# First expert's tokens found by one-hot products, tables joined on GpSimd, put-off sums and a third sum at other steps

## The chip, the cores and the metric

The kernel runs on one core of a Trainium2 chip. TensorE (PE) multiplies, VectorE (DVE) and ScalarE (ACT) move and combine, GpSimd (POOL) does a little arithmetic and issues indirect DMAs, SP issues most plain DMAs. The metric is the device time of one execution in microseconds (us). The median of the runs and their spread are given; one execution was also recorded by the profiler, and all rows below are of that one.

## The reference

Three stages in a row, all in float32. `q`, `k`, `v` are (4, 8, 576, 64), so 2304 tokens of width 512.

```python
# 1. windowed causal attention with a distance bias, 8 heads, window 128
scores = where(mask, q @ k.T / 8 + bias, -1e9)
x = softmax(scores) @ v                         # tokens x 512
# 2. a gated layer, d_ff 1536
x = (sigmoid(x @ w_gate) * (x @ w_val)) @ w_out
# 3. eight experts, each token goes to one
logits = normalize(x) @ normalize(expert_emb).T / tau
expert_idx = argmax(logits); gate_w = softmax(logits)[expert_idx]
for e in range(8):
    m = expert_idx == e
    out[m] = gate_w[m] * (relu(x[m] @ w1[e]) @ w2[e])   # 512 -> 1024 -> 512
```

## The kernel before, in words

**Precision.** Every matmul operand is split into a high part in a short float format and the rest: ScalarE casts the high part (`hi_copy`, line 106), VectorE subtracts it to get the low part (`lo_sub`, line 122), and TensorE does three products (high x high, high x low, low x high). So each weight tile of 128x1024 costs a cast of some 1.05 us on ScalarE and a subtraction of some 1.22 us on VectorE before TensorE can use it.

**Attention and the gated layer.** Attention runs in 36 units, and the gated layer follows in two groups of token blocks (`PAIRS`, called the first and the second group here) for which the products with the weights use a seven-product scheme: sums S1 to S4 of blocks of x, and T1 to T4 of the weights, replace one product in eight. `builds(pair)` makes the sums and their splits: `"S3+"` computes the third sum of the second group (`sum_x`, line 332, one VectorE operation on 128x1024), `"S3"` splits it. `seven(pair, f, ...)` gives the products m1 to m7 of one of the twelve column blocks f with what follows each of them. The result g is not used at once: `keep_g` multiplies gate and value (line 484), stores the blocks A11 to A22 of g to memory and also forms sums of them (S1 to S4, line 465) for the products with `w_out`. Where such a sum isn't needed at once, it is put off: a closure goes into `put_off`, and `catch_up(n, pin)` takes the next one out, computes it on VectorE and stores it (`put`: on SP's queue for the first group, on GpSimd's for the second). Until it is stored, the rows that it reads and writes stay taken. At the end of the first group some sums are left over; the loop over f of the second group (line 883) takes one out after `m3` of each of its first three steps.

**Rows.** Most temporaries of 128x513 floats (`row(name)`) come from one pool `mid` of ten buffers: gate and value blocks, the converted `w_out` (`cvwo`), the routed rows `xr`, the gathered rows `xg`, the results `y`. An instruction that writes a new row waits until the last use of an older one is over, and with a store or a gather that means until the DMA has landed.

**The output product and the routing.** 14 products (`SEQ`) form x2 = g @ w_out, group by group; beside TensorE's work, `AT2` lists what is issued at which step (j, half z, place). As soon as a group of token blocks is ready, it is routed. The groups are b = 3, 5, 1, 7 (four blocks of 128 tokens each) and 0 (two blocks); 7 and 0 are called `LATE`.
- `route_a`, `route_l` compute the logits, the maximum, its index (`ixf`), the softmax weight (written into column 512 of the row, line 1061), and GpSimd writes the rows to `x2_d` in memory (line 1063).
- `route_b` (line 1071) gives each token its place among those of its expert: matmuls of a one-hot `oh` with a triangle of ones (`rk`), then `rank`; from it the address `ai` (line 1095) in a table. GpSimd then scatters the token numbers `ids_sb` to that address by an indirect DMA for each block (line 1102), into one of four tables `tab_d[u]` (u is the block in the group), so that the four scatters don't wait for each other. An empty entry holds the number NT = 2304, above all tokens.
- `places(o, x, c0, q)` reads a column range of all four tables by four DMAs on queue q and joins them by two VectorE operations `min` (lines 954 and 955): an empty entry loses against a token. The result is a list of token numbers.
- `gather` (line 1145) fetches the listed rows of `x2_d` by an indirect DMA on GpSimd. With `upto` it leaves out numbers from there on and the row is cleared first (line 1150).
- `close` runs after `route_b(1)`: it counts the tokens, picks the most loaded expert but the first as second (`by_count`; SP and GpSimd read its number into a register), and then, for expert 0 (two tiles of 128 tokens) and the second one (one tile), calls `places` and `gather`. These first tiles hold tokens of groups 3, 5 and 1 only, so the experts can begin before the groups 7 and 0 are routed; `bump` makes the ranks of the late groups begin behind them.

**The experts.** `transp` turns gathered rows (`tx`), `ffn1` and `ffn2` are the two products, and each result is scattered to the output by an indirect DMA on GpSimd. Expert 0 starts with its two early tiles while groups 7 and 0 are still being routed. After `route_b(0)` the weights of the second expert are converted (`weights(1)`), and `load_col(0)`, `load_col(1)` read the rest of both lists from the tables (into `more`, then `cols`); then come the gathers of these tiles, and from there the experts in turn, each with the next one's weights loaded and converted beside it.

**Order.** Inside `tc.manual_schedule` blocks the listed engines work in the order of the text. Outside, the builder's planner orders the instructions of each engine from their dependences and its own estimates of time; `tc.issue_after(i)` holds instructions until after i in that order, `tc.keep_in_program_order` pins one. At run time every engine, and each of the two queues SP and GpSimd, works strictly in the planned order: an instruction that waits holds up all behind it.

Of the kernel before, what the change touches and what calls it, by code (L numbers as in the profile page):

```python
# [9 lines left out]
F32 = mybir.dt.float32  # L10
F32R = mybir.dt.float32r
BF16 = mybir.dt.bfloat16
# [11 lines left out]
DM = 512  # L24
# [36 lines left out]
def attn_ffn_moe(ctx: ExitStack, tc: tile.TileContext, qkd, vd, wgv, w_out, emb, tau, w1, w2, cst, ids, out):  # L61
# [10 lines left out]
    tab_d = [dram.tile([P * E * TCOL, 1], I32, tag=f"tab_d{y}", name=f"tab_d{y}") for y in range(NTAB)]  # L72
# [21 lines left out]
    tri_f = cs[:, P:2 * P]  # L94
# [522 lines left out]
    nc.sync.dma_start(cs, cst[:, 8 * P:])  # L617
# [214 lines left out]
    bB["S2"]()  # L832
    split_w(1, 0, 1)
    run(2)
    load_wt(1)
# [44 lines left out]
    bB["S3+"]()  # L880
    bB["S3"]()
    WO_AT = [[], [0], [1], [2], [3], [4], [5, 6], [7], [8], [9], [10], []]
    for f in range(KF):
# [6 lines left out]
        if f == 0:  # L890
            bB["A22"]()
            bB["S4+"]()
            bB["S4"]()
# [14 lines left out]
        if f == KF - 1:  # L908
            split_op(0, [0, 1])
        s["m3"]()  # L910
        if f < 3:
            catch_up(pin=True)
# [32 lines left out]
    idt = cp.tile([P, E * TCOL], I32, tag="idt", name="idt")  # L945
    nc.gpsimd.memset(idt, NT)
# [4 lines left out]
    def places(o, x, c0, q):  # L951
        for y, v in enumerate(tab_v):
            q.dma_start(x[:, y, :], v[:, bass.ds(c0, o.shape[1])])
        nc.vector.tensor_tensor(out=x[:, 0:2, :], in0=x[:, 0:2, :], in1=x[:, 2:4, :], op=ALU.min)
        nc.vector.tensor_tensor(out=o, in0=x[:, 0, :], in1=x[:, 1, :], op=ALU.min)
# [9 lines left out]
    tri = cp.tile([P, P], BF16, tag="tri", name="tri")  # L965
    nc.vector.tensor_copy(tri, tri_f)
    one = cp.tile([P, P], BF16, tag="one", name="one")
# [14 lines left out]
    cp.tile([P, 16], I32, tag="pad", name="pad")  # L982
    idx0 = cp.tile([P, 2 * CE], I32, tag="idx0", name="idx0")
    idxs = [cp.tile([P, NTAB, n], I32, tag=f"idxs{e}", name=f"idxs{e}") for e, n in enumerate(EARLY)]
    routed, mark, reg, held = {}, {}, {}, {}
# [85 lines left out]
    def route_b(b):  # L1071
# [13 lines left out]
        nc.vector.tensor_reduce(out=rank, in_=j8, axis=mybir.AxisListType.X, op=ALU.add)  # L1085
        ri = few(nu, "ri", f"ri{b}", dt=I32)
# [13 lines left out]
        for u in range(nu):  # L1100
            t = 2 * b + u
            nc.gpsimd.indirect_dma_start(out=tab_d[u], out_offset=IOA(ap=ai[:, u:u + 1], axis=0),
                                         in_=ids_sb[:, t:t + 1], in_offset=None)
# [24 lines left out]
    def close():  # L1128
# [8 lines left out]
        for e, n in enumerate(EARLY):  # L1137
            reg[e] = nc.gpsimd.value_load(ord_e[0:1, e:e + 1], min_val=0, max_val=E - 1) if e else 0
            places(idx0[:, e * CE:e * CE + n], idxs[e], reg[e] * TCOL, nc.gpsimd)
            for t in range(n):  # L1140
                gather(e, t, idx0[:, e * CE + t:e * CE + t + 1], NE * P)

    xg = {}
# [289 lines left out]
    route_b(0)  # L1433
    behind(0, lambda: weights(1))()
# [17 lines left out]
    for e in range(2):  # L1452
        load_col(e)
# [210 lines left out]
```

## Time and profile before

| what | value |
|---|---|
| runs | 822.89 us median of 3 (819.43 to 824.91) |
| profiled execution | 825.32 us, span of its instructions 823.6 us |
| TensorE busy | 786.6 us (96%), mean granted clock 0.975 |
| VectorE busy | 583.2 us (71%) |
| ScalarE busy | 449.1 us (55%) |
| GpSimd busy | 216.9 us (26%) |
| DMA | 175.77 MB, mean 213 GB/s |

The span is from the first to the last instruction. A granted clock of 1.00 is TensorE's full 2.4 GHz, 0.50 is 1.2 GHz, and a mean over a stretch lies between. PEld is the load of weights into TensorE, which runs beside its products. A row of a timeline gives the start, the length, engine, line, operation, output and inputs by their names in the program, and in brackets the idle time just before it and what ended that.

### The profile page before, as it was taken

To read this page: it belongs to the slowest core of one execution; us is meant where nothing else is said; L and a number is where in the kernel's file an instruction comes from. 1 tells how busy PE (TensorE), PEld (TensorE's weight loads), DVE (VectorE), ACT (ScalarE), POOL (GpSimd) and SP (SyncE) were. 2 spreads that over 40 slices of the span, in tenths; PEclk is the share of its full clock that TensorE was granted. 3 is DMA by queue.
4 is the path that set the end of the run, shared out by engine and by line. 5 is a ranking of instruction groups with operands and counts; after the bars stand their busy time and mean duration, and the time that the engine had idled before them with its cause. 6 is when DMAs were issued, how large, how long until landed. Compare 5 with 4: busy or idle time off the path is not lost. (4 is left out here: it accounts for less than half of the span.)

```text
span 823.6 us, 15796 instructions
## 1 busy us (share of the span) xinstructions
PE 786.6 (96%) x5585; PEld 657.7 (80%) x5585; DVE 583.2 (71%) x1372; ACT 449.1 (55%) x953; POOL 216.9 (26%) x346
## 2 busy tenths in 40 slices
PE   8989999999999889999999999969799999999996
PEld 5768888878888668887787777748579989899995
DVE  7988978889899768897877587618355785456621
ACT  6888766666546445556656677536143543344510
POOL 6756423322000012232200033533503120402100
PEclk9998999999999899999999999979899999999999
DMA  8686478865674489999985596475448745636100
GB/s 273 202 260 218 148 255 280 272 230 195 239 250 172 173 326 352 355 363 377 342 273 181 161 242 207 117 179 129 104 138 295 234 169 184 212 103 229 57 24 19
DMA packets 75714, 175.77 MB, mean 213 GB/s; under 512 B 12499, under 2 KB 20819, under 8 KB 75632
## 3 DMA queue, kind: packets, MB, share of 16 engines
q1 hardware_dynamic: 65264, 145.24, 53.0%
q0 software_dynamic: 10368, 29.50, 10.5%
q8 instruction: 45, 0.74, 0.4%
q14 instruction: 37, 0.30, 0.1%
HBM read 120.95 MB, written 54.45 MB: 213 GB/s over the span
## 5 line engine op out<-in xcount | busy, mean ns | idle before, releaser
L1187 PE MATMUL h<-xe,weh 128*128 128x256 f32 (+4 forms) x512 | 105.8, 300 | 0.0
L118 POOL TENSOR_SCALAR p<-p,rs 128x192 f32<-128x192 f32 x140 | 76.4, 563 | 93.3 <-DVE rs L269 53.0
L122 DVE TENSOR_TENSOR wel<-wer,weh 128x1024 fp32r<-128x1024 f32 x64 | 76.9, 1222 | 20.1 <-PE zt L1222 9.7
L1187 PEld LDWEIGHTS h<-xe,weh 128*128 128x128 f32 x512 | 84.0, 189 | 1.8 <-issue 0.4
L253 ACT ACTIVATE p<-p,mx 128x192 f32<-128x192 f32 x144 | 64.0, 446 | 27.8 <-DVE mx L250 27.7
L1187 PE MATMUL h<-xe,wel 128*128 128x256 f32 (+4 forms) x256 | 76.6, 299 | 0.0
L1205 PE MATMUL z<-weh,h 128*128 128x512 f32 (+1 forms) x224 | 72.2, 401 | 0.2 <-ACT h L1189 0.2
L1189 ACT ACTIVATE h<-h 128x256 fp32r<-128x256 f32 (+4 forms) x64 | 26.7, 417 | 76.7 <-PE h L1187 75.1
L106 ACT CAST weh<-wer 128x1024 fp32r<-128x1024 f32 x64 | 65.7, 1048 | 4.4 <-PE z L1205 2.1
L1190 DVE SCALAR_TENSOR_TENSOR h<-h,h 128x256 fp32r<-128x256 f32 (+4 forms) x64 | 29.6, 464 | 42.8 <-ACT h L1189 42.7
L122 DVE TENSOR_TENSOR ol<-ol,oh 128x1024 fp32r<-128x1024 f32 x42 | 49.8, 1220 | 9.6 <-ACT oh L106 9.6
L1205 PEld LDWEIGHTS z<-weh,h 128*128 128x128 f32 (+1 forms) x224 | 41.5, 190 | 9.3 <-ACT h L1189 0.6
L1187 PEld LDWEIGHTS h<-xe,wel 128*128 128x128 f32 x256 | 48.6, 190 | 0.1
L1205 PE MATMUL z<-wel,h 128*128 128x512 f32 (+1 forms) x112 | 44.8, 400 | 0.0
L1310 PE MATMUL b<-oh,wo 128*128 128x512 f32 x144 | 44.4, 390 | 0.0
L106 ACT CAST oh<-ol 128x1024 fp32r<-128x1024 f32 x42 | 41.4, 1048 | 0.0
L1210 POOL DMA_INDIRECT out<-y,cols x13 | 12.9, 993 | 101.5 <-DVE y L1209 62.4
L1310 PE MATMUL b<-oh,th 128*128 128x512 f32 x96 | 38.2, 401 | 0.0
L1310 PE MATMUL b<-oh,tl 128*128 128x512 f32 x96 | 38.1, 397 | 0.0
L1310 PE MATMUL b<-ol,th 128*128 128x512 f32 x96 | 37.9, 395 | 0.0
L239 PE MATMUL s<-qk 64*64 64x128 f32 (+2 forms) x864 | 34.8, 282 | 1.4 <-DVE mx L250 0.7
L1209 DVE TENSOR_SCALAR y<-z,xg 128x512 f32<-128x512 f32 (+1 forms) x16 | 12.0, 747 | 34.1 <-PE z L1205 34.1
(482 smaller groups left out, 2223.4 us busy)
## 6 DMA issues: line engine op xcount, KB each, us to landing
wer<-in_w SPq DMA_DIRECT2D x64, 512.0 KB, 5.1
wr<-in_wgv SPq DMA_DIRECT2D x24, 512.0 KB, 5.9
qk<-in_qkd SPq DMA_DIRECT2D x36, 320.0 KB, 3.9
v<-in_vd SPq DMA_DIRECT2D x36, 192.0 KB, 3.6
wor<-in_w_out SPq DMA_DIRECT2D x12, 512.0 KB, 7.0
ol<-g0S SPq DMA_DIRECT2D x12, 512.0 KB, 7.7
ol<-g1S SPq DMA_DIRECT2D x12, 512.0 KB, 6.3
wq_d<-wh SPq DMA_DIRECT2D x10, 512.0 KB, 2.8
```

The source lines that it names most:

```text
L106: nc.scalar.copy(o, i)
L118: nc.gpsimd.tensor_scalar(out=t, in0=t, scalar1=r, scalar2=0.0, op0=ALU.mult, op1=ALU.add)
L122: e.tensor_tensor(out=o, in0=i, in1=h.bitcast(F32), op=ALU.subtract)
L239: nc.tensor.matmul(ss[u][y * 64:(y + 1) * 64, j * WK + d:j * WK + d + n], q[halves[u], a:a + 64], k[halves[u], a + c0:a + c0 + n], start=T ...
L253: nc.scalar.activation(out=o, in_=o, func=AF.Exp, scale=-1.0, bias=mx[:, z:z + 1], accum_out=su[:, z:z + 1])
L1187: nc.tensor.matmul(m[:, :n], w[:, fs], x[:, k, :], start=(cnt == 0), stop=(cnt == 3 * KD - 1))
L1189: nc.scalar.activation(out=hh, in_=m[:, :n], func=AF.Relu)
L1190: nc.vector.scalar_tensor_tensor(out=hl, in0=m[:, :n], scalar=0.0, in1=hh.bitcast(F32), op0=ALU.max, op1=ALU.subtract)
L1205: nc.tensor.matmul(m[0:w, :], h, ww[:, ds], start=(cnt == 0), stop=(cnt == 3 * KE - 1))
L1209: nc.vector.tensor_scalar_mul(y[0:w, :], m[0:w, :], x[0:w, DM:DM + 1])
L1210: nc.gpsimd.indirect_dma_start(out=out, out_offset=IOA(ap=idx[0:w], axis=0), in_=y[0:w, :], in_offset=None, bounds_check=NT - 1, oob_is_er ...
L1310: nc.tensor.matmul(bk[pair, z], p, q, start=(first and kk == 0 and y == 0), stop=(kk == KF // 2 - 1 and y == 2), skip_group_check=True)
```

## The change

Four things are changed.

1. *First expert.* In `route_b` of the groups 3, 5 and 1 (`if b not in LATE`), VectorE compares `ixf * 2 NT + rank` with the numbers 0 to 255: for each of the four blocks and each of the two tiles one comparison of 128x128, which gives a one-hot matrix `place` (a row of the pool `mid`, as bf16). TensorE multiplies these with two columns `tkc` (block number + 1 and place in the block), eight matmuls of two columns, and VectorE adds the result to `found`. After group 1, three small VectorE operations turn `found` into the token numbers `idx0` (2304 for an empty place), and the two gathers of expert 0 are issued there, ahead of the scatters of group 1 in the program. `close` reads tables for the second expert's tile only.
2. *Tables.* They hold floats: token number less NT, and 0 for an empty entry. `places` adds the four tables and then NT by three operations on GpSimd, where there were two minima on VectorE. The reads of `load_col(0)` and `load_col(1)` are issued only after the last scatter of group 0; both are on GpSimd's queue.
3. *Put-off sums.* The three left-over sums of the first group are all taken out in step f = 0 of the second group: behind `S4+`, ahead of `m3`, behind `m3`.
4. *Third sum.* `S3+` and `S3` of the second group are called between earlier products (after `S2`, and two products later) and no longer after `m1`, `m2` of step 0.

The triangle for the ranks moves out of the constants loaded at the start into a row that is loaded later, and a row of numbers 0 to 127 takes its place there.

```diff
@@ -830,8 +830,10 @@
     split_w(1, 0, 0)
     run(2)
     bB["S2"]()
+    bB["S3+"]()
     split_w(1, 0, 1)
     run(2)
+    bB["S3"]()
     load_wt(1)
     load_wo(0)
...
@@ -877,8 +879,6 @@
     sv = [seven(1, f, "mts", False) for f in range(KF)]
     sv[0]["m1"]()
     sv[0]["m2"]()
-    bB["S3+"]()
-    bB["S3"]()
     WO_AT = [[], [0], [1], [2], [3], [4], [5, 6], [7], [8], [9], [10], []]
     for f in range(KF):
         s, t = sv[f], sv[f + 1] if f + 1 < KF else None
@@ -890,6 +890,7 @@
         if f == 0:
             bB["A22"]()
             bB["S4+"]()
+            catch_up(pin=True)
             bB["S4"]()
         if t:
             t["m1"]()
@@ -907,8 +908,10 @@
             load_wo(KF - 1)
         if f == KF - 1:
             split_op(0, [0, 1])
+        if f == 0:
+            catch_up(pin=True)
         s["m3"]()
-        if f < 3:
+        if f == 0:
             catch_up(pin=True)
         if KF - 3 <= f < KF - 1:
             load_op(f - KF + 3)
...
-    idt = cp.tile([P, E * TCOL], I32, tag="idt", name="idt")
-    nc.gpsimd.memset(idt, NT)
+    idt = cp.tile([P, E * TCOL], F32, tag="idt", name="idt")
+    nc.gpsimd.memset(idt, 0.0)
     tab_v = [t.rearrange("(p c) o -> p (c o)", p=P) for t in tab_d]
     for t in tab_v:
         nc.sync.dma_start(t, idt)
@@ -951,8 +954,9 @@
     def places(o, x, c0, q):
         for y, v in enumerate(tab_v):
             q.dma_start(x[:, y, :], v[:, bass.ds(c0, o.shape[1])])
-        nc.vector.tensor_tensor(out=x[:, 0:2, :], in0=x[:, 0:2, :], in1=x[:, 2:4, :], op=ALU.min)
-        nc.vector.tensor_tensor(out=o, in0=x[:, 0, :], in1=x[:, 1, :], op=ALU.min)
+        nc.gpsimd.tensor_tensor(out=x[:, 0:2, :], in0=x[:, 0:2, :], in1=x[:, 2:4, :], op=ALU.add)
+        nc.gpsimd.tensor_tensor(out=x[:, 0, :], in0=x[:, 0, :], in1=x[:, 1, :], op=ALU.add)
+        nc.gpsimd.tensor_scalar_add(o, x[:, 0, :], float(NT))
...
 
     tri = cp.tile([P, P], BF16, tag="tri", name="tri")
+    tri_r = row("tri_f")
+    tri_f = tri_r[:, 0:P]
+    nc.sync.dma_start(tri_f, cst[:, 8 * P + NCST:])
     nc.vector.tensor_copy(tri, tri_f)
+    tkc = cp.tile([P, NBLK, 2], BF16, tag="tkc", name="tkc")
+    part_of = tri_r[:, P:P + NBLK].bitcast(I32)
+    for z, (op, by) in enumerate(((ALU.arith_shift_right, 7), (ALU.bitwise_and, P - 1))):
+        nc.vector.tensor_scalar(out=part_of, in0=ids_sb, scalar1=by, scalar2=None, op0=op)
+        if z == 0:
+            nc.vector.tensor_scalar_add(part_of, part_of, 1)
+        nc.vector.tensor_copy(tkc[:, :, z], part_of)
+    ids_f = cp.tile([P, NBLK], F32, tag="ids_f", name="ids_f")
+    nc.vector.tensor_scalar_add(ids_f, ids_sb, -float(NT))
+    found = cp.tile([P, CE, 2], F32, tag="found", name="found")
+    nc.vector.memset(found, 0.0)
...
-    idxs = [cp.tile([P, NTAB, n], I32, tag=f"idxs{e}", name=f"idxs{e}") for e, n in enumerate(EARLY)]
-    routed, mark, reg, held = {}, {}, {}, {}
+    idxs = cp.tile([P, NTAB, 1], F32, tag="idxs", name="idxs")
+    routed, mark, reg, held, xg = {}, {}, {0: 0}, {}, {}
...
@@ -1083,6 +1100,32 @@
             nc.tensor.matmul(o, tri, oh[:, u, :], start=False, stop=True, skip_group_check=True)
         nc.vector.tensor_tensor(out=j8, in0=rk[:, 0:nu * E].rearrange("p (u e) -> p u e", u=nu), in1=oh, op=ALU.mult)
         nc.vector.tensor_reduce(out=rank, in_=j8, axis=mybir.AxisListType.X, op=ALU.add)
+        if b not in LATE:
+            r0 = few(nu, "r0", f"r0{b}")
+            nc.vector.scalar_tensor_tensor(out=r0, in0=ixf, scalar=float(2 * NT), in1=rank, op0=ALU.mult, op1=ALU.add)
+            place = row(f"place{b}")[:, 0:DM].bitcast(BF16)
+            for u in range(nu):
+                for c in range(CE):
+                    z = u * CE + c
+                    nc.vector.tensor_scalar(out=place[:, z * P:(z + 1) * P], in0=iota128, scalar1=float(c * P),
+                                            scalar2=r0[:, u:u + 1], op0=ALU.add, op1=ALU.is_equal)
+            fd = rk[:, 256:256 + 2 * CE]
+            for u in range(nu):
+                for c in range(CE):
+                    z = u * CE + c
+                    nc.tensor.matmul(fd[:, 2 * c:2 * c + 2], place[:, z * P:(z + 1) * P], tkc[:, 2 * b + u, :],
+                                     start=(z == 0), stop=(u == nu - 1), skip_group_check=True)
+            nc.vector.tensor_tensor(out=found, in0=found, in1=fd.rearrange("p (c k) -> p c k", c=CE), op=ALU.add)
+        if b == 1:
+            empty = few(CE, "r0", "empty")
+            nc.vector.tensor_scalar(out=empty, in0=found[:, :, 0], scalar1=0.0, scalar2=float(NT + P), op0=ALU.is_equal,
+                                    op1=ALU.mult)
+            tok_f = few(CE, "ad", "tok_f")
+            nc.vector.scalar_tensor_tensor(out=tok_f, in0=found[:, :, 0], scalar=float(P), in1=found[:, :, 1], op0=ALU.mult,
+                                           op1=ALU.add)
+            nc.vector.scalar_tensor_tensor(out=idx0[:, 0:CE], in0=tok_f, scalar=-float(P), in1=empty, op0=ALU.add, op1=ALU.add)
+            for t in range(CE):
+                gather(0, t, idx0[:, t:t + 1], NE * P)
         ri = few(nu, "ri", f"ri{b}", dt=I32)
         rl = few(nu, "rl", f"rl{b}", dt=I32)
         rh = few(nu, "rh", f"rh{b}", dt=I32)
@@ -1100,7 +1143,7 @@
         for u in range(nu):
             t = 2 * b + u
             nc.gpsimd.indirect_dma_start(out=tab_d[u], out_offset=IOA(ap=ai[:, u:u + 1], axis=0),
-                                         in_=ids_sb[:, t:t + 1], in_offset=None)
+                                         in_=ids_f[:, t:t + 1], in_offset=None)
...
         nc.vector.tensor_scalar_max(bump[0:1, :], lim, 0.0)
-        for e, n in enumerate(EARLY):
-            reg[e] = nc.gpsimd.value_load(ord_e[0:1, e:e + 1], min_val=0, max_val=E - 1) if e else 0
-            places(idx0[:, e * CE:e * CE + n], idxs[e], reg[e] * TCOL, nc.gpsimd)
-            for t in range(n):
-                gather(e, t, idx0[:, e * CE + t:e * CE + t + 1], NE * P)
-
-    xg = {}
+        reg[1] = nc.gpsimd.value_load(ord_e[0:1, 1:2], min_val=0, max_val=E - 1)
+        places(idx0[:, CE:CE + 1], idxs, reg[1] * TCOL, nc.gpsimd)
+        gather(1, 0, idx0[:, CE:CE + 1], NE * P)
...
     hs = ffn1(0, CE * P, between={0: [lambda: route_a(0, *late, now=False)], 1: [lambda: route_l(0), lambda: we0(5)], 2: [lambda: we0(6)], 4: [lambda: we0(7)]})
     route_b(0)
+    last_scatter = latest(ENG.Pool)[0]
     behind(0, lambda: weights(1))()
...
         t0 = EARLY[e] if e < len(EARLY) else 0
         nt = -(-CAPS[e] // P) - t0
         cols[e] = cp.tile([P, nt], I32, tag=f"cols{e}", name=f"cols{e}")
-        other = cp.tile([P, NTAB, 3], I32, tag=f"more{e % 2}", name=f"more{e}")[:, :, 0:nt]
+        other = cp.tile([P, NTAB, 3], F32, tag=f"more{e % 2}", name=f"more{e}")[:, :, 0:nt]
         places(cols[e], other, reg.get(e, order[e]) * TCOL + t0, nc.gpsimd if e in reg else nc.sync)
 
     def col(e, t):
         t -= EARLY[e] if e < len(EARLY) else 0
         return cols[e][:, t:t + 1]
 
-    for e in range(2):
-        load_col(e)
+    with tc.issue_after(last_scatter):
+        for e in range(2):
+            load_col(e)
     by_count(cps, msk, 2, E - 2)
```

## Rows read from the trace of the kernel before

**Rows 1.** Stretches: length, busy us (instructions) by engine, granted clock, DMA share, GB/s.

```profile
268.00:284.00 16.00, 13.38 (x43) 9.60 (x41) 12.70 (x17) 7.94 (x11) 0.00 (x0) 0.79 0.59 218
296.00:308.00 12.00, 9.22 (x35) 7.20 (x34) 7.88 (x12) 4.49 (x8) 2.75 (x6) 0.86 1.02 386
460.00:540.00 80.00, 79.83 (x433) 63.06 (x433) 53.60 (x168) 53.02 (x104) 28.43 (x31) 1.00 0.69 196
523.00:529.00 6.00, 6.00 (x32) 5.04 (x31) 5.96 (x18) 0.94 (x2) 5.26 (x3) 1.00 0.01 0
541.00:558.00 17.00, 9.15 (x34) 7.03 (x34) 5.52 (x26) 6.23 (x10) 5.29 (x7) 0.60 0.50 107
561.80:562.20 0.40, 0.40 (x17) 0.40 (x17) 0.38 (x1) 0.40 (x3) 0.00 (x0) 1.00 0.00 0
585.00:601.00 16.00, 9.22 (x37) 6.79 (x36) 4.79 (x9) 3.05 (x5) 7.54 (x10) 0.79 0.27 81
```

**Rows 2.** TensorE's waits over the whole run: total us, times, longest us.

```profile
PE tx L1167 <- DMA xg<-x_d,idx: 6.1, 2, 5.1
PE ht L1246 <- DVE wel L122: 5.4, 1, 5.4
```

**Rows 3.** Timeline of VectorE, 258 to 275 us: start, length, instruction [idle before, releaser].

```profile
260.86 1.23 DVE L122 TENSOR_TENSOR xl_(1, 'S1')_3895<-xq_(1, 'S1')_3884,xh_(1, 'S1')_3894 128x1024 fp32r<-128x1024 f32 x1 [1.56 <-ACT xh_(1, 'S1')_3894 L106]
...
273.54 1.23 DVE L122 TENSOR_TENSOR xl_(1, 'S3')_3998<-xq_(1, 'S3')_3995,xh_(1, 'S3')_3997 128x1024 fp32r<-128x1024 f32 x1 [1.11 <-ACT xh_(1, 'S3')_3997 L106]
```

**Rows 4.** Timeline of all engines, 298.2 to 301 us.

```profile
298.37 0.32 SPq L460 DMA_DIRECT2D g0S<-r  x1
...
300.88 0.66 ACT L126 ACTIVATE cvwo<-wor 128x512 f32<-128x512 f32 x1 [5.88 <-issue]
```

**Rows 5.** Timeline of GpSimd, 523 to 553 us.

```profile
525.18 0.96 POOL L1102 DMA_INDIRECT tab_d<-ids_sb,ai  x1 [0.30 <-issue]
526.44 2.99 POOL L1102 DMA_INDIRECT tab_d<-ids_sb,ai  x1 [0.30 <-DVE kte L1121]
...
531.55 2.17 POOL L1063 DMA_DIRECT2D x_d<-xr  x4
...
547.16 1.07 POOL L1151 DMA_INDIRECT xg<-x_d,idx  x1 [4.18 <-DVE idx L955]
```

**Rows 6.** Timeline of VectorE, 523 to 552 us.

```profile
525.21 0.33 DVE L1061 RECIPROCAL xr<-sx 128x1 f32<-128x1 f32 x4
...
545.99 0.16 DVE L954 TENSOR_TENSOR idxs<-idxs 128x4 int32<-128x4 int32 x1 [15.45 <-DMA idxs<-tab_d]
```

**Rows 7.** DMA issues, 529 to 556 us: count, KB each, median us to landing.

```profile
x_d<-xr POOLq DMA_DIRECT2D x4, 256.5 KB, 10.6
...
xg<-x_d,idx POOLq DMA_INDIRECT x3, 3.3
```

**Rows 8.** Costliest groups by shape, VectorE and GpSimd: busy us, mean ns, idle before.

```profile
L122 DVE TENSOR_TENSOR xe<-tx,xe 128x128 fp32r<-128x128 f32 x1 | 0.3, 292 | 2.9 <-ACT xe L106 2.9
...
L170 POOL TENSOR_SCALAR bias<-relm 128x256 f32<-128x256 f32 x6 | 2.5, 420 | 3.6 <-DMA relm<-in_cst 3.5
```

**Rows 9.** Timeline of all engines, 574 to 601 us.

```profile
574.81 0.16 DVE L1095 SCALAR_TENSOR_TENSOR ai<-ixf,ad 128x2 int32<-128x2 f32 x1
...
577.22 1.09 POOL L953 DMA_DIRECT2D more<-tab_d  x2 [3.90 <-DMA tab_d<-ids_sb,ai]
...
580.81 0.99 POOL L1102 DMA_INDIRECT tab_d<-ids_sb,ai  x1 [0.30 <-issue]
...
587.70 0.16 DVE L954 TENSOR_TENSOR more<-more 128x2 int32<-128x2 int32 x1 [6.82 <-DMA more<-tab_d]
...
589.62 1.00 POOL L1148 DMA_INDIRECT xg<-x_d,cols  x1 [0.30 <-DVE more L954]
589.64 2.38 DVE L122 TENSOR_TENSOR wel<-wer,weh 128x1024 fp32r<-128x1024 f32 x2
...
600.40 0.66 PE L1167 MATMUL tx<-cs,xg 128*128 128x128 f32 x4 [0.91 <-DVE hk L122]
```

More of the change, by code (lines that the diff above doesn't have):

```diff
@@ L71, in attn_ffn_moe @@
     x2_d = dram.tile([NT + 1, DM + 1], F32, tag="x2_d", name="x2_d")
-    tab_d = [dram.tile([P * E * TCOL, 1], I32, tag=f"tab_d{y}", name=f"tab_d{y}") for y in range(NTAB)]
+    tab_d = [dram.tile([P * E * TCOL, 1], F32, tag=f"tab_d{y}", name=f"tab_d{y}") for y in range(NTAB)]
     wf_d = dram.tile([KF * P, 2 * KD * P], F32, tag="wf_d", name="wf_d")
@@ L93, in attn_ffn_moe @@
     ident = cs[:, 0:P]
-    tri_f = cs[:, P:2 * P]
+    iota128 = cs[:, P:2 * P]
     iota8 = cs[:, 256:264]
@@ L616, in attn_ffn_moe @@
     load_qk(2)
-    nc.sync.dma_start(cs, cst[:, 8 * P:])
+    nc.sync.dma_start(cs, cst[:, 8 * P:8 * P + NCST])
     load_v(0)
@@ L981, in attn_ffn_moe @@
     nc.vector.memset(bump, 0.0)
-    cp.tile([P, 16], I32, tag="pad", name="pad")
     idx0 = cp.tile([P, 2 * CE], I32, tag="idx0", name="idx0")
-    idxs = [cp.tile([P, NTAB, n], I32, tag=f"idxs{e}", name=f"idxs{e}") for e, n in enumerate(EARLY)]
-    routed, mark, reg, held = {}, {}, {}, {}
+    idxs = cp.tile([P, NTAB, 1], F32, tag="idxs", name="idxs")
+    routed, mark, reg, held, xg = {}, {}, {0: 0}, {}, {}
     def few(n, tag, name, *shape, dt=F32):
@@ L1587, in attn_ffn_moe @@
         ix = sm.tile([P, 1], I32, tag="ovix", name="ovix")
-        places(ix, sm.tile([P, NTAB, 1], I32, tag="ovjx", name="ovjx"), cv, nc.sync)
+        places(ix, sm.tile([P, NTAB, 1], F32, tag="ovjx", name="ovjx"), cv, nc.sync)
         X = E
@@ L1615, in _constants @@
     tri = (np.arange(P)[:, None] < np.arange(P)[None, :]).astype(np.float32)
+    places = np.tile(np.arange(P, dtype=np.float32), (P, 1))
     iota = np.tile(np.arange(MAXOV, dtype=np.float32), (P, 1))
@@ L1619, in _constants @@
     fold = np.tile(np.eye(P // KD, E, dtype=np.float32), (KD, 1))
-    cst = np.concatenate([relm, np.eye(P, dtype=np.float32), tri, iota, tail, fold], axis=1)
+    cst = np.concatenate([relm, np.eye(P, dtype=np.float32), places, iota, tail, fold, tri], axis=1)
     ids = (np.arange(NBLK)[None, :] * P + np.arange(P)[:, None]).astype(np.int32)
```

## The prediction, made before the change was run

> **What bounds the kernel now.** I read the page first: TensorE is busy for 786.6 of 823.6 us, so a gain can come only from the 37 us in which it stands still and from the stretches in which it runs at the lower of its two clocks. So the next view is the table of stretches [rows 1], and for each stretch I take *lost time = idle time + busy time x (1 - granted clock)*. Four stretches matter. 268 to 284 us: 2.62 + 13.38 x 0.21 = 5.4 us. 296 to 308: 2.78 + 9.22 x 0.14 = 4.1. 541 to 558: 7.85 + 9.15 x 0.40 = 11.5. 585 to 601: 6.78 + 9.22 x 0.21 = 8.7. Together 29.7 us. Between 460 and 540 TensorE is busy for 79.83 of 80 us: what the change adds there on other engines is hidden as long as it is not late, what it adds on TensorE is paid in full. TensorE's waits [rows 2] name the causes: the gathered rows `xg` (6.1 us) and the converted weights `wel` (5.4); the other two stretches are read from other engines' rows.
>
> Each has a story in the rows. **541 to 558:** VectorE stood still for 15.45 us on the table reads, until 545.99 [rows 6], and only then could GpSimd gather at 547.16 [rows 5]. **585 to 601:** VectorE waited again, 6.82 us, for the tables `more`; the two `wel` conversions of expert 1 that TensorE needed stand behind that wait in VectorE's order and ran at 589.64 [rows 9]. **296 to 308:** ScalarE waited 5.88 us for a buffer of the ring of rows, until 300.88; the put-off sum `r` had been stored at 298.37 [rows 4], and behind it in ScalarE's order stands the copy `r` that TensorE needs next. **268 to 284:** VectorE converted the third sum only at 273.54, after a wait of 1.11 us, and had stood idle for 1.56 us at 259.3 [rows 3].
>
> **The change part by part.**
>
> *Third sum sooner.* No work is added. The sum (1.22 us) needs only attention outputs that are long there, and fits the 1.56 us of idle VectorE; the 1.11 us wait for ScalarE's cast goes too. VectorE is otherwise full in this stretch, so the gain is bounded by 2.67 us of its idle time if the clock behaves as before, and by 5.4 if nothing waits any more; it is 0 if other work that is now pushed back (the `wl` split) becomes late by the same amount. I take 2.0.
>
> *Put-off sums of the first group.* Three sums move from the ends of steps 0, 1, 2 into step 0. Each also issues a store on SP. The rows that they hold are then free some 290 us into the run, before ScalarE wants one at 295.0 (300.88 - 5.88), so the wait goes. What it costs: 2 x 0.7 us of VectorE earlier, in a stretch in which it is busy for 12.70 of 16 us [rows 1], so they fit; and on SP, whose queue waits in order, the stores stand ahead of weight loads, which a late sum would hold up. I take 3.5 of the 4.1 us (0 if another row holds the ring).
>
> *First expert's tokens by products.* Each of three routed groups gets eight comparisons of 128x128 on VectorE (nearest row: 0.29 us for that size [rows 8]; 2.3 us), two or three small operations (0.16 each [rows 6]), and eight matmuls of two columns. 17 bf16 matmuls of this kind began in 0.4 us [rows 1]; eight are 0.2 us if they pipeline like that, and I take 0.25, three times 0.25 = 0.7 us on TensorE in full. VectorE's 3 x 2.8 = 8.4 us lie in 460 to 540, where it is idle for 26 of 80 us: hidden behind TensorE's full work, but for late evictions, for which I put 0.5.
>
> In return no table is read for expert 0 and no minimum waits on VectorE. What is late next? The gather needs the rows of group 1 in memory. Their last operand was ready at 525.54 [rows 6], but the writes were issued at 531.55, behind four scatters, among them one of 2.99 us [rows 5]. Now the rank chain, and so the scatters, come some 2.5 us later, and the gathers stand ahead of the scatters in the program, so I expect the writes first, at 524.6 to 527, when the DMA engines were idle (share 0.01 in 523 to 529 [rows 1]). They then land by 530 or so; the gathers follow between scatters at 530 to 533, into a stretch in which the writes took 10.6 us [rows 7]. Landing is then between 534 (3.3 us after the issue, the gathers' median [rows 7]) and 543. TensorE has other work in this part until about 545, so little need be left: I keep 3 us of the 11.5 and take 8.5 (all of it at best, 4 if the writes stay where they were, rival 1). The next in line is expert 1's first tile, still read from tables: GpSimd's queue of writes, scatters, gathers and reads reaches it at about 547, and TensorE needs it at about 553 now.
>
> *Tables joined by additions of GpSimd.* Three small operations on GpSimd in place of two on VectorE for each read. No row shows so small an operation on GpSimd; 0.42 us is the row of a 128x256 one [rows 8]. Three are 0.3 to 1.3 us; I take 0.7, as an element-wise operation on 4 columns is nearer to a fixed cost. What counts is the place of the wait: it now blocks GpSimd, where gathers that need the result come next anyway, and no longer VectorE, where `wel` stood. So the 5.41 us wait for `wel` goes. Then the gathered rows are next: before, two reads ran at 577.22 ahead of the last scatters, whose operand was ready at 574.97; the scatters ended at 581.80, gathers began at 589.62 [rows 9]. With the reads held until after the last scatter, the scatters start at about 575.2 and end at 578. From their end to the gather 7.8 us passed before (landing, six reads, two minima); to these come two more reads of 0.55 and 0.7 us for the additions, so the gather is issued at about 587.7 and its rows are there, 3.3 us later, at 591. Without the wait for `wel` and the slow clock TensorE would be there at 600.40 - 5.41 - 1.94 = 593. The two times are close, so I take 6.0 of the 8.7 us (3 if the gathers land 3 to 4 us later, 8 at best).
>
> **A rule against it.** In 523 to 529 VectorE was busy for 5.96 of 6 us [rows 1]; a scatter that began there at 526.44 held GpSimd for 2.99 us, another, at 525.18, for 0.96 [rows 5]. So an operation of GpSimd can take 2 us more beside a busy VectorE. The Trainium skill (SBUF — State Buffer, Who interferes with whom) says that a VectorE instruction with two SBUF inputs contends with a GpSimd instruction that reads SBUF, and that the later one fully blocks; by that rule each addition on GpSimd could wait for a conversion of VectorE, and the time would be that of rival 3. The rows bear on scatters alone; no row here shows an addition on GpSimd.
>
> *Other.* The triangle is loaded later, by a DMA of its own, and some eight small VectorE operations (0.16 us each) prepare the token numbers before the products of pairs begin; the first group that needs them is routed 80 us later. I cost both at nothing; if they came late, the first rank would wait, and with it scatters that nothing waits for until 541.
>
> **The sum.** 2.0 + 3.5 + 8.5 - 0.7 - 0.5 + 6.0 = 18.8 us. The profiled execution took 825.3 us, so 806.5; the median of the runs is 822.9, 2.4 less, so I predict 804 (times below are against the median too). Bounds of the terms: all at their best 5.4 + 4.1 + 11.5 + 8.0 - 0.7 = 28.3 (795), all at their worst 0 + 0 + 4 + 3 - 1.2 = 5.8 (817), which would take every one at once.
>
> **Rivals.**
> (1) *The gather still waits for the written rows* ("it doesn't find them sooner in effect"). If the writes stay behind the four scatters, they land at about 542 (531.55 + 10.6), the gathered rows come at about 547, some 4 us before the 550.5 of now (547.16 + 3.3): 4 us instead of 8.5, so 808.5. For it: the writes were ready at 525.5 and still went last. Against: the scatters' operands now come later.
> (2) *VectorE is the bound of the first part*: 12.70 of 16 us busy at 268 to 284, and full before; the moved sums then only push others back and the ring is held by another row. 5.5 us less: 809.5.
> (3) *GpSimd's additions wait for VectorE.* At 2.99 - 0.96 = 2.0 us for each of three additions, 6 us in the last stretch: its gain is gone, 810. Against: VectorE is idle for 11 of 16 us there.
> (4) *Slower: the products stall TensorE.* In each of three groups TensorE must wait, in its own order, for VectorE's eight comparisons, in a part where it is now full. A wait costs double: 2.62 us of idle time came with a loss of 5.4 in 268 to 284. Three waits of 4.5 us would be 28 us, against a gain of 19: 832. It decides from waits of 3 us each (3 x 3 x 2.1 = 19). For it: VectorE is in order and full in 523 to 529 (5.96 of 6 us). Against: elsewhere in 460 to 540 TensorE lost 0.17 us with the same kind of round trip in it.
>
> **How the numbers follow.** Forecast 804: 0.54. Rival 1: 0.17. Rival 2: 0.11. Rival 3: 0.09. Rival 4: 0.07. The rest, 0.02, is a gain near the best of all terms. The range 795 to 816 holds the best sum, the first three rivals, and two of them at once (804 + 4.5 + 5.5 = 814); left out are rival 4 and nearly all terms at their worst. A difference under 1%, 8 us, is about what a measurement of this kernel cannot tell from none. Faster by more than that (under 814.7): forecast and rivals 1 to 3 but for the cases in which they come together, 0.82. Within 1%: 0.11, those cases. Slower: 0.07.
>
> **What the profile would show.** Right: no wait of VectorE on `idxs` or `more`; the writes of group 1 ahead of its scatters on GpSimd; TensorE's lost time in the stretch of the first expert at 3 us or less, in that of expert 1 under 3, the clock at full between; ScalarE's `cvwo` without the 5.88 us wait; TensorE without a wait for the third sum. Wrong: a wait of TensorE for `xg` of several us (rival 1), for `place` (rival 4), for `wl` or `xl` in the first part (rival 2), additions of over 1 us on GpSimd (rival 3). The prediction would fail most by a wait for expert 1's first tile, or by GpSimd's queue, in which table reads now block the scatters and gathers behind them.

## The result and the profile after

The changed kernel takes 811.1 us (median of its runs, 810.0 to 814.6) against 821.5 of the kernel before in the same rounds: ratio 0.9877, 95% interval 0.9829 to 0.9925. It is faster by 10 us, where 18.8 were forecast. Its profiled execution took 810.75 us, with a span of 809.1.

First the stretches of [rows 1], in the changed kernel (length, busy time of TensorE, its weight loads, VectorE, ScalarE and GpSimd, then TensorE's clock, DMA share and GB/s):

```profile
268.00:284.00 16.00, 12.91 (x46) 8.67 (x44) 13.46 (x18) 7.90 (x11) 0.00 (x0) 0.89 0.41 119
296.00:308.00 12.00, 12.00 (x54) 9.91 (x54) 10.81 (x19) 5.54 (x10) 3.60 (x7) 1.00 1.02 401
460.00:540.00 80.00, 79.75 (x431) 59.74 (x430) 58.84 (x200) 49.16 (x94) 28.55 (x32) 1.00 0.64 201
541.00:558.00 17.00, 15.03 (x107) 12.03 (x106) 11.61 (x52) 14.88 (x35) 5.46 (x10) 0.90 0.48 154
585.00:601.00 16.00, 15.30 (x82) 12.12 (x83) 8.76 (x11) 8.11 (x13) 1.02 (x1) 1.00 0.54 155
```

By the measure of the prediction (idle time plus busy time times the missing clock) the four stretches now lose 3.09 + 12.91 x 0.11 = 4.5 us, 0, 3.5 and 0.7: together 8.7 where it was 29.7. So 21.0 us of loss went from these stretches, and the forecast counted on 20.0. They are the same in time but not in work: the changed kernel is 8 us ahead at the first transposition of a gathered row (542.9 us, before 551.0) and 14.5 at the end. Over the whole span TensorE stood idle for 823.6 - 786.6 = 37.0 us before and 809.1 - 785.4 = 23.7 after. Its waits agree in kind. The two of [rows 2], on `xg` and `wel`, are gone; behind the attention part three of 1 us or more are left besides the copies `r` and `c`, the first two of them new (total, times, longest):

```profile
PE a L439 <- ACT wh L106: 2.0, 1, 2.0
PE rk L1095 <- DVE acc L1142: 1.4, 1, 1.4
PE tx L1206 <- DVE hk L122: 1.0, 1, 1.0
```

GpSimd's timeline in place of [rows 5] (start, length, instruction, idle before it and what ended it):

```profile
524.08 2.21 POOL L1080 DMA_DIRECT2D x_d<-xr  x4 [10.04 <-DVE rh L1136]
...
529.64 2.56 POOL L1145 DMA_INDIRECT tab_d<-ids_f,ai  x1 [0.31 <-issue]
532.50 1.19 POOL L1190 DMA_INDIRECT xg<-x_d,idx  x1 [0.30 <-issue]
...
535.73 1.04 POOL L1190 DMA_INDIRECT xg<-x_d,idx  x1 [0.30 <-issue]
...
542.62 0.20 POOL L957 TENSOR_TENSOR idxs<-idxs 128x2 f32<-128x2 f32 x1 [2.48 <-DMA idxs<-tab_d]
542.90 0.20 POOL L958 TENSOR_TENSOR idxs<-idxs 128x1 f32<-128x1 f32 x1
543.19 0.24 POOL L959 TENSOR_SCALAR idx<-idxs 128x1 int32<-128x1 f32 x1
```

The writes of the rows go first, and the first expert's gathers are issued at 532.5 and 535.7, with nothing read from a table. The additions take 0.2 us each.

Where, then, did the rest go? TensorE was busy for all of the stretch in which the products of pairs run, before and after, but it needs longer for it. I cut every trace at the first matmul of the second group, the first product of a pair (`b<-oh`), the first output product (`y<-wo`) and the first transposition of a gathered row (`tx`). In us:

| kernel | A: to group 2 | B: to pairs | C: to output | D: to `tx` | E: to the end |
|---|---|---|---|---|---|
| before | 264.73 | 130.75 | 129.71 | 25.82 | 272.61 |
| changed | 265.34 | 125.89 | 134.73 | 16.98 | 266.15 |

The clock was at full in C, before and after. C became 5.0 us longer; the prediction has 1.2 for that. Of the 24 matmuls of two columns 16 stand singly there and eight in pairs, so in 20 places. TensorE's timeline in the changed kernel:

```profile
521.70 0.39 PE L1349 MATMUL b<-oh,tl 128*128 128x512 f32 x1
521.92 0.39 PE L1349 MATMUL b<-ol,th 128*128 128x512 f32 x1
522.15 0.39 PE L1349 MATMUL b<-oh,th 128*128 128x512 f32 x1
522.38 0.18 PE L1116 MATMUL rk<-tkc,place 128*128 128x2 bf16 x1
522.42 0.47 PE L1349 MATMUL b<-oh,tl 128*128 128x512 f32 x1
522.73 0.18 PE L1116 MATMUL rk<-tkc,place 128*128 128x2 bf16 x1
522.77 0.47 PE L1349 MATMUL b<-ol,th 128*128 128x512 f32 x1
```

What counts is the distance of starts, not the modelled length. Large to large is 0.22 to 0.23 us; small to large is 0.04, but from that large one to whatever is next it is 0.31. So a product that stands alone costs 0.36 - 0.23 = 0.13 us. I took all 24 to stand alone, 3.1 us; with the four that follow another small one at 0.03, it is 20 x 0.13 + 4 x 0.03 = 2.7. That leaves some 2 us in C without a reason, and it does not grow where groups are routed: it is there from the first products on, some 80 us ahead of the first one-hot matmul. The pace of ordinary matmuls has changed, so I looked at what the diff did to the place of tiles in SBUF.

### The profile page after: what moved, and what is told of

The parts are those of the page before. It is cut to its first block, busy times and chain, and to the rows that moved or that the text cites. A ratio compares the mean times of both kernels' runs of the same rounds, so it can differ in the third digit from the quotient of the medians.

```text
span 809.1 us, 15897 instructions
## 1 busy us (share of the span) xinstructions
PE 785.4 (97%) x5608; PEld 653.1 (81%) x5609; DVE 586.7 (73%) x1392; ACT 451.4 (56%) x955; POOL 224.3 (28%) x369
## 5 line engine op out<-in xcount | busy, mean ns | idle before, releaser
L1080 POOL DMA_DIRECT2D x_d<-xr x18 | 10.0, 563 | 110.9 <-ACT th L106 68.8
```

Source lines behind the costliest of these rows:

```text
L1080: nc.gpsimd.dma_start(x2_d[t0:t0 + P, :], xr[u])
```

## The experiments

The tiles of the left side of SBUF begin behind the constants. The diff drops a pad of 64 bytes and a table of indices, and adds `tkc`, `ids_f` and `found`. By the two programs' addresses the left side begins 128 bytes later; the right side (the `wo` halves, tiles of the output stage) stayed. Before, nearly all large operands lay at 192 modulo 256 bytes; after the change those of the left side lie at 64. Theory 1: that costs TensorE time.

**The kernel before, its left side moved by 128 bytes.** In the line of the pad:

```
-    cp.tile([P, 16], I32, tag="pad", name="pad")
+    cp.tile([P, 48], I32, tag="pad", name="pad")
```

> The kernel before with its pad 128 bytes longer (192 instead of 64): every tile of the left side of SBUF moves by 128 bytes, as in the changed kernel, and every engine's order of instructions stays what it was. Theory 1 (where the tiles lie): a matmul of 512 columns after which weights are loaded from the other 128-byte half of a 256-byte block takes 232 ns to the next one and not 227. The shift brings 638 thousand columns into that position where 88 thousand stood, so 550 thousand / 512 x 5.2 ns = 5.6 us more: 827 against 821.5. Rival 2 (the one-hot products and their surroundings cost everything that is missing): the place of tiles does nothing, 821.5 within 1 us.

Measured: 824.3 us, ratio 1.0031 (1.0016 to 1.0046): slower by 2.5 us, with every engine's order unchanged. C is 130.87 us, 1.16 more. The pace shows in TensorE's timeline, first the kernel before:

```profile
400.69 0.39 PE L1310 MATMUL b<-ol,wo 128*128 128x512 f32 x1
400.92 0.61 PE L1310 MATMUL b<-oh,wo 128*128 128x512 f32 x2
401.37 0.39 PE L1310 MATMUL b<-ol,wo 128*128 128x512 f32 x1
401.60 0.61 PE L1310 MATMUL b<-oh,wo 128*128 128x512 f32 x2
402.05 0.39 PE L1310 MATMUL b<-ol,wo 128*128 128x512 f32 x1
```

and the same products with the shift:

```profile
400.88 0.40 PE L1310 MATMUL b<-ol,wo 128*128 128x512 f32 x1
401.12 0.62 PE L1310 MATMUL b<-oh,wo 128*128 128x512 f32 x2
401.59 0.39 PE L1310 MATMUL b<-ol,wo 128*128 128x512 f32 x1
401.82 0.62 PE L1310 MATMUL b<-oh,wo 128*128 128x512 f32 x2
402.28 0.40 PE L1310 MATMUL b<-ol,wo 128*128 128x512 f32 x1
```

Six matmuls take 402.05 - 400.69 = 1.36 us, and 402.28 - 400.88 = 1.40: 227 and 233 ns each, at the full clock. Joining successive 128x512 matmuls of a trace, where none waits, with the addresses of what they read gives (moving operand, then the weights of the next matmul, modulo 256 bytes; number of pairs; median distance of starts):

```
before             192, 192: 1760, 227 ns   192,  64:  36, 232 ns
shifted by 128      64,  64: 1121, 227 ns    64, 192: 634, 232 ns   192,  64:  50, 232 ns
shifted by 64        0,   0: 1084, 227 ns     0, 192: 632, 229 ns   192,   0:  50, 233 ns   0, 64: 36, 233 ns
changed             64,  64: 1104, 227 ns    64, 192: 636, 232 ns   192,  64:  62, 232 ns
changed, matched   192, 192: 1770, 227 ns   192,  64:  36, 232 ns
```

Theory 1 stands, at half of its price: the whole lost 2.5 us (1.3 to 3.8), not 5.6. The table gives the smaller price: with the shift 634 + 50 - 36 = 648 more pairs take 232 ns, 648 x 5 ns = 3.2 us. The 5.6 counted narrower matmuls at the same price per column, and joined in the same way these two traces show next to none for them (median at the same place, then 128 bytes apart): 120 and 119 ns for 256 columns, 147 and 148 for 320, 173 and 175 for 384.

**The kernel before, moved by 64 bytes.** The pad is 32 columns wide.

> The kernel before with its pad 64 bytes longer, so that the tiles of the left side lie at 0 of 256 bytes and those of the right side at 192; every engine's order is what it was. Theory 1a (what counts is which 128-byte half the two operands lie in): the same columns as with the shift of 128 bytes are opposed, 232 ns, 824.3. Theory 1b (what counts is the distance, and 64 bytes are half as bad or nothing): 227 to 230 ns, 821.5 to 823.

Measured: ratio 0.9989 (0.9963 to 1.0014), no difference; most of the pairs that don't match take 229 ns in the table above. So theory 1a falls: 0 and 192 lie in opposite halves and lose 2 ns, not 5. 1b holds for them, but not for the few pairs whose weights lie 64 bytes above (0 and 64, 192 and 0), which take 233. What exactly counts beside the match stays open; that a match takes 227 holds in all five traces.

**The changed kernel with its tiles where they were.** 128 bytes of constants are saved:

```
-    tau_t = cp.tile([P, 1], F32, tag="tau", name="tau_t")
-    itau = cp.tile([P, 1], F32, tag="itau", name="itau")
+    tau2 = cp.tile([P, 2], F32, tag="tau", name="tau_t")
+    tau_t, itau = tau2[:, 0:1], tau2[:, 1:2]
...
-    ids_f = cp.tile([P, NBLK], F32, tag="ids_f", name="ids_f")
+    ids_f = ids_sb[:, :].bitcast(F32)
```

> The changed kernel with 128 bytes of constants saved on the left side of SBUF (the token numbers converted in place, two one-column tiles in one), so that the tiles lie as before the change; no work is added or left out. Theory 1 (where the tiles lie): 5.5 us less than the changed kernel, 805.5 against 811; between the first product of a pair and the first output product, 134.7 us become 133. Rival 2 (the one-hot products cost everything that is missing): 811 within 1.5 us, and that stretch stays at 134.7.

Measured: 807.0 us, ratio 0.9827 (0.9805 to 0.9850) where the change has 0.9877: 4.1 us better. The change's own interval is 4 us wide to either side, so this amount is known to some 4 us only, and the same holds for every difference to the change below. Traces give less noise in C, where the clock was at full: C is 133.59, 1.14 shorter, the same amount as the shift added to the kernel before.

**The one-hot matmuls of a group in a row.**

```
-            for u in range(nu):
-                for c in range(CE):
-                    z = u * CE + c
-                    nc.tensor.matmul(fd[:, 2 * c:2 * c + 2], place[:, z * P:(z + 1) * P], tkc[:, 2 * b + u, :],
-                                     start=(z == 0), stop=(u == nu - 1), skip_group_check=True)
+            for n, z in enumerate(reversed(range(nu * CE))):
+                u, c = divmod(z, CE)
+                i = nc.tensor.matmul(fd[:, 2 * c:2 * c + 2], place[:, z * P:(z + 1) * P], tkc[:, 2 * b + u, :],
+                                     start=(n == 0), stop=(u == 0), skip_group_check=True)
+                if n:
+                    tc.keep_in_program_order(i)
```

> The changed kernel with the eight one-hot matmuls of a group issued one right behind the other (last comparison first, so that none starts before all are there). Theory 3 (a one-hot matmul that stands singly between large ones costs 0.13 us, 24 of them 3.1 us, in a row 0.03 to 0.05): the stretch from the first product of a pair to the first output product becomes 2 to 2.5 us shorter, 132.5 us, and the whole 808.8. Rival 4 (they cost the same wherever they stand): 134.7 and 811. Rival 5 (TensorE now waits for the last comparison, and the switch is no cost): a wait of up to 1 us for the comparisons in each group, the whole 811 to 814.

Measured: 809.1 us, ratio 0.9847 (0.9822 to 0.9872); C is 133.00, 1.73 shorter. By C theory 3 holds, a little below its size, since only 20 switches were there to go; the times alone, 809.1 and 811.1, differ by less than their intervals. No wait for the comparisons appears. **With both edits:**

> The changed kernel with both edits: tiles as before the change, and the eight one-hot matmuls of a group in a row. Theories 1 and 3 together: 811 - 5.5 - 2.3 = 803, which is where the sum of the prediction stands. Theory 1 alone: 805.5. Theory 3 alone: 808.8. Neither: 811.

Measured: 805.3 us, ratio 0.9795 (0.9772 to 0.9818); C is 131.78, 2.95 shorter, the sum of the two (1.14 + 1.73 = 2.87). This kernel is faster than the kernel before and than the changed one. Its timeline where the products stood singly:

```profile
522.56 0.39 PE L1350 MATMUL b<-oh,th 128*128 128x512 f32 x1
522.78 0.39 PE L1350 MATMUL b<-oh,tl 128*128 128x512 f32 x1
523.01 0.35 PE L1115 MATMUL rk<-tkc,place 128*128 128x2 bf16 x8
523.23 0.48 PE L1350 MATMUL b<-ol,th 128*128 128x512 f32 x1
523.55 0.40 PE L1350 MATMUL b<-oh,th 128*128 128x512 f32 x1
```

Eight take 0.22 us, and the 0.32 after a switch is paid once: 0.3 us for a group instead of some 0.9 (2.7 / 3).

**Without the one-hot matmuls.**

```
-            fd = rk[:, 256:256 + 2 * CE]
...
-                    nc.tensor.matmul(fd[:, 2 * c:2 * c + 2], place[:, z * P:(z + 1) * P], tkc[:, 2 * b + u, :],
-                                     start=(z == 0), stop=(u == nu - 1), skip_group_check=True)
-            nc.vector.tensor_tensor(out=found, in0=found, in1=fd.rearrange("p (c k) -> p c k", c=CE), op=ALU.add)
...
-    nc.vector.memset(found, 0.0)
+    nc.vector.memset(found, 1.0)
```

> The changed kernel without the one-hot matmuls; the comparisons on VectorE stay, and the first expert's rows are those of one fixed token, so its part of the result is not computed. The stretch from the first product of a pair to the first output product. Theory 3 (the matmuls themselves and the switch to and from them): 134.7 - 3.1 = 131.6 us or a little less. Rival (the comparisons make evictions late, or change the order around them): 134 or more.

Measured (one execution, 808.6 us): C is 131.74, so the matmuls cost 2.99 us of the 5.02.

**The first expert's tokens from the tables again**, joined on GpSimd. The comparisons, the products and the block that makes tokens of `found` are gone, and the second expert's reads use the free tile `found`:

```
-        places(idx0[:, CE:CE + 1], idxs, reg[1] * TCOL, nc.gpsimd)
+        places(idx0[:, 0:CE], idxs, 0, nc.gpsimd)
+        for t in range(CE):
+            gather(0, t, idx0[:, t:t + 1], NE * P)
+        places(idx0[:, CE:CE + 1], found.rearrange("p c (k o) -> p (c k) o", o=1), reg[1] * TCOL, nc.gpsimd)
```

> The changed kernel with the first expert's tokens read from the tables again, joined on GpSimd; no comparisons and no one-hot matmuls. The prediction's terms: 8.5 us lost to the gathered rows come back, 1.2 of TensorE are saved: 818 against 811. By what the runs before show of the products' price (3.9 us between the first product of a pair and the first output product): 8.5 - 3.9 = 4.6, 815.7. Rival (joining on GpSimd alone frees the first expert too, the products bring nothing): 807, faster than the change.

Measured: 817.8 us, ratio 0.9957 (0.9936 to 0.9978), so this part of the change is worth 0.0080 of 821, 6.6 us net. TensorE's wait is back:

```profile
PE tx L1183 <- DMA xg<-x_d,idx: 8.3, 2, 7.6
```

C is 130.79 us, D + E are 293.48 against 283.13: the products give 10.3 us behind the first output product and take 3.9 ahead of it. With the run above, C is accounted for: 129.71 before, 1.16 by the place of tiles, 2.99 by the matmuls, and 131.74 - 130.79 = 0.95 by the comparisons and what they change in the order; together 134.81, and it was 134.73. The rival (GpSimd's joining alone frees the first expert) falls.

**The tables joined on VectorE again** (`nc.vector` for the three additions).

> The changed kernel with the additions that join the tables on VectorE again (two additions and one of the offset, in the same place). The prediction's theory (what counts is that the wait for the reads no longer stands in VectorE's order, ahead of the conversions): a wait of VectorE for the reads of 5 to 7 us and one of TensorE for the converted weights come back, 6 us more, 817 against 811. Rival (holding the reads behind the scatters did it, not the engine): 811.

Measured: 816.3 us, ratio 0.9931 (0.9909 to 0.9954): this part is worth 0.0054, 4.4 us. VectorE's timeline, and a row of TensorE's:

```profile
542.99 0.16 DVE L957 TENSOR_TENSOR idxs<-idxs 128x2 f32<-128x2 f32 x1 [9.79 <-DMA idxs<-tab_d]
...
575.12 0.16 DVE L957 TENSOR_TENSOR more<-more 128x2 f32<-128x2 f32 x1 [3.99 <-DMA more<-tab_d]
```

```profile
577.58 0.50 PE L1285 MATMUL ht<-wel,xe 128*128 128x512 f32 x1 [2.10 <-DVE wel L122]
```

Both waits stand in VectorE's order again, and the conversion `wel` behind the second is late for TensorE by 2.1 us (5.4 in [rows 2]). D + E are 286.95 us against 283.13, 3.8 more. So the engine that waits matters, with the order of the reads unchanged. The size is loose: with one and the same order of instructions TensorE's wait for `wel` was 5.4 us in the trace of the kernel before, 6.0 in that of the shift by 128 bytes and 2.2 in that of the shift by 64.

**The reads not held behind the last scatter** (the block `tc.issue_after(last_scatter)` removed).

> The changed kernel without the order that holds the reads of the tables behind the last scatter: two reads of the later experts' tables stand ahead of the last writes and scatters on GpSimd, as before the change. The prediction's theory (the two reads delay the scatters, with them the other reads, the additions and the gather of the second expert by 1 to 2 us, and TensorE waits for its rows or weights): 812 to 814 against 811. Rival (GpSimd has slack there): 811.

Measured: 810.6 us, ratio 0.9889 (0.9859 to 0.9918), no difference to the change within the intervals; E is 266.18 and was 266.15. GpSimd has slack there, and no gain of this line of the diff shows.

**The first part alone**: third sum and put-off sums in the kernel before.

> The kernel before with the third sum sooner and the put-off sums of the first group inside step 0, and nothing else of the change. The prediction's terms: 2.0 + 3.5 = 5.5 us, 816 against 821.3. Theory 6 (the lost time of the two stretches was in part the lower clock of that one execution: up to the first product of a pair the two executions with the old first part lost 8.5 and 1.7 us to the clock, and their second stretches were 130.8 and 128.7 us long, those with the new one 125.0 to 127.4): about 3.5 us, 818. Rival (VectorE is the bound there): 821.

Measured: 818.6 us, ratio 0.9953 (0.9935 to 0.9971): 3.9 us (2.4 to 5.3). **And the third sum alone:**

> The kernel before with the third sum sooner alone. The prediction's term: 2.0 us, 819.5. Theory 7 (its two waits of TensorE, 1.8 and 0.8 us, go, and a wait of 1.5 to 2.0 us for the converted weights that were pushed back behind it takes their place, as in the runs with both edits): 0.6 to 1.1 us, 820.5; the wait of 2.3 to 2.8 us for the copy behind the ring of rows stays. Rival (nothing takes its place): 2.6 us and no wait for the weights.

Measured: 823.2 us, ratio 1.0038 (1.0018 to 1.0057): not faster, if anything slower by 1.5 to 4.7 us. TensorE's waits between 262 and 400 us, first in the shifted kernel (whose order is that of the kernel before), then with the third sum moved:

```profile
PE a L439 <- ACT r L562: 3.0, 2, 2.3
PE a L439 <- ACT xh_(1, 'S3')_3997 L106: 1.8, 1, 1.8
PE a L439 <- ACT c L569: 0.9, 2, 0.7
PE a L439 <- DVE xl_(1, 'S3')_3998 L122: 0.8, 1, 0.8
PE a L439 <- DVE wt L122: 0.5, 1, 0.5
```

```profile
PE a L439 <- ACT r L562: 3.9, 3, 2.5
PE a L439 <- ACT wh L106: 1.7, 1, 1.7
PE a L439 <- ACT c L569: 0.9, 2, 0.7
PE a L439 <- DVE wt L122: 0.7, 1, 0.7
```

The waits for the third sum (1.8 + 0.8) go; one for the converted weights `wh` (1.7) comes, and those for `r` and `wt` grow by 0.9 and 0.2: together 7.0 us before and 7.2 after. VectorE is busy for 14.2 of 16 us there (268 to 284) in both traces, ScalarE for 7.7 and 8.4; why the cast `wh` is late was not followed further. With the put-off sums moved too, the wait for `r` falls to 1.4. **Last, the best kernel with the third sum at its old place:**

> The changed kernel with its tiles as before the change and the one-hot matmuls in a row, and with the third sum at its old place, so that of the first part only the put-off sums are moved. Theory 7 (the third sum's move is worth nothing: its two waits of 2.6 us go, waits of 1.7 to 2.4 us for converted weights come): 805 to 806, as with the move. Theory 8 (by the run with the third sum alone, which was 0.4% slower than the kernel before, the move costs 2 to 4 us): 802. The prediction's term: 2.0 us more, 807.3.

Measured: 805.5 us, ratio 0.9827 (0.9801 to 0.9853), against 805.3 and 0.9795 (0.9772 to 0.9818) with it moved; the kernel before had a lower median in that set of runs (819.1), and the two intervals overlap. Theory 8 finds no support. Alone the third sum's move cost time, in the best kernel it did not: no run shows a gain by it that is clear of the intervals.

## Why the prediction was right in kind and its gain 8 us too large

The ways were those forecast, and the time lies between the forecast (804) and the top of its range (816). By its own steps:

- *Lost time.* 20.0 us of the 29.7 were to go and 21.0 went, some of it by the clock alone (below). No wait on `idxs` or `more` stands in VectorE's order, the writes go ahead of the scatters at 524.08 (forecast 524.6 to 527), the gathers at 532.5 and 535.7 (530 to 533 and after), the waits for `xg`, `wel` and `cvwo` are gone.
- *First expert's tokens, what it brings*: 8.5 forecast, 10.3 in the trace of the run without it. It came out better: TensorE found the rows there and did not wait for them at all. A wait of 1.4 us for `acc` is new behind them, so 541 to 558 still loses 3.5 us, where the prediction's sign was 3 or less.
- *First expert's tokens, what it costs*: the term that was mis-sized. Forecast 0.7 + 0.5 = 1.2 us; measured 3.9 (2.99 for the matmuls, 0.95 with the comparisons). I priced a matmul of two columns by 17 small ones in a row [rows 1], and most of these stand singly between large ones. The row of a series gives the price in a series; the switch back costs 0.09 us each time.
- *Other*, "I cost both at nothing": here is the step that failed outright. I looked at the new constants for their work and their readiness, not for what they push. They and the dropped pad move the left side by 128 bytes: 4.1 us (known to some 4) by the run that matches the tiles again, 2.5 (1.3 to 3.8) by the one that shifts them in the kernel before.
- *Third sum* 2.0: no gain measured. The prediction named the case (0 if the work that is pushed back becomes late by the same amount) and didn't choose it, though VectorE's row had it nearly full. *Put-off sums* 3.5: with the third sum together 3.9, so by these runs the gain of the first part is theirs; they were not run alone in the kernel before.
- *Tables joined on GpSimd* 6.0: measured 4.4, within some 4. The wait of 5.4 us from which the term was taken varies by nearly 4 us between executions of one order, as said above, so a closer forecast from one trace would have been luck.

Added up from the single runs: 3.9 + 4.4 + 6.6 - (2.5 to 4.1) = 10.8 to 12.4 us, where the whole gave 0.0123 x 821 = 10.1. The 3.9 and the 2.5 are known to some 1.5 us, the three that are differences to the change (4.4, 6.6 and 4.1) to some 4 each, so the agreement is not closer than that.

The trace of before made the gain look larger, too: that execution took 825.3 us, 3.9 above the median, and ran its first 395 us at a clock of 0.99 and 0.96 (to 264 us, and from there), the shifted kernel at 1.00 and 0.99 in the same order of instructions. In 268 to 284 us the shifted kernel has 3.3 us of idle time at a clock of 1.00, where the trace of before has 2.6 at 0.79: so 2.8 of the 5.4 us read there as loss by a wait was this execution's clock. Of B's 130.75 us too, the shifted kernel needs 128.69.

The rivals. (1) did not happen: the writes went first. (2) happened by half: the third sum's move only pushed others back, as the wait for `wh` shows, but the ring of rows came free. (3) shows once in the changed kernel, and TensorE has no wait for it: two operations of GpSimd took 1.05 and 1.08 us beside four conversions of VectorE that began at 625.54, where those of the first experts took 0.20 to 0.24.

```profile
627.60 0.36 POOL L957 TENSOR_TENSOR more<-more 128x6 f32<-128x6 f32 x1
628.04 1.05 POOL L958 TENSOR_TENSOR more<-more 128x3 f32<-128x3 f32 x1
629.17 1.08 POOL L959 TENSOR_SCALAR cols<-more 128x3 int32<-128x3 f32 x1
```

```profile
625.54 4.63 DVE L122 TENSOR_TENSOR wel<-wer,weh 128x1024 fp32r<-128x1024 f32 x4 [0.26 <-ACT weh L106]
```

The Trainium skill (SBUF — State Buffer, Who interferes with whom) says that a VectorE instruction with two inputs in SBUF contends with a GpSimd instruction that reads SBUF; the two rows agree, at about the length of one of the four conversions (4.63 / 4 = 1.16 us). In the run with the one-hot matmuls in a row three such operations ran beside conversions `xe`, one of whose two inputs lies in PSUM, and took 0.19, 0.19 and 0.24 us, so not every conversion delays them. (4) did not happen: TensorE never waited for the comparisons. Its price for a wait, double the idle time, was read from 268 to 284 us, and there the lower clock did not come with the wait, as the shifted kernel shows.

## What to carry to other kernels

An edit that adds or drops a small constant moves every tile behind it: compare the addresses of the large operands of TensorE before and after, modulo 256 bytes, when its pace has changed; here that was worth 2.5 us of 821. Price a small matmul by its neighbours: between large ones it costs a switch each (0.13 us here), in a row it is nearly free (0.3 us for eight), so issue small ones together. Where an engine is nearly full, moving one of its steps ahead may only choose which other step is late, as with the third sum. Read a wait from more than one execution before you put a price on it.

## What the runs showed of the hardware

- At full clock a 128x512 fp32r matmul followed by one whose weights lie at the same place modulo 256 bytes as its moving operand took 227 ns to the next start; with weights 128 bytes off 232, 64 bytes below 229, 64 above (86 pairs) 233. With 648 more such pairs at 128 bytes, by a shift that left every order as it was, a kernel of 821 us was 2.5 us slower. Narrower matmuls showed little of it: 147 and 148 ns for 320 columns, 173 and 175 for 384.
- After a bf16 matmul of two columns a large one took 0.31 to 0.32 us to the next start instead of 0.23; eight small ones in a row took 0.22 us. Whether the type or the width makes the switch was not tried.
- An addition of GpSimd on 128x1 to 128x6 elements took 0.19 to 0.24 us, and up to 1.08 beside conversions of VectorE that read two tiles in SBUF.
